# The order of the first loads, and the order of the work, in a gated SSM and MLP kernel with all its gradients

## The chip, the cores and the metric

The kernel runs on one core of a Trainium2 chip, in one launch. The metric is the device time of that launch in microseconds (us), here as the median of several runs. A core has five instruction streams: TensorE (PE, matmuls, with its weight loads shown as PEld), VectorE (DVE), ScalarE (ACT), GpSimd (POOL) and SyncE (SP). Each works through its own list in order. SP, ACT and POOL also issue DMA transfers, each into a queue of its own: SP's is q1, ACT's q10 and POOL's q0 in the profile.

## The reference, cut to what matters

```python
# u: 1 x 2048 x 448, bf16; A, B, C: 448 x 256 complex (six real arrays); w1: 448 x 1792
g = sigmoid((u * gate_w).sum(-1, keepdims=True))
# S4: kernel of the state space model, then a causal convolution over the 2048 steps
dt = exp(log_dt)
K  = einsum("dn,dnl,dn->dl", C, exp(dt * A * l), dt * B).real     # l = 0 .. 2047
a  = irfft(rfft(pad(u)) * rfft(pad(K)))[:2048] + u * Dskip
# MLP with a squared ReLU
b  = relu(u @ w1 + b1) ** 2 @ w2 + b2
out = g * a + (1 - g) * b
# and jax.vjp of out for grad_out: gradients of u, the six parameters, log_dt, Dskip, w1, b1, w2, b2, gate_w
```

The output and the 14 gradients are all written.

## The kernel before

The program is recorded first and ordered afterwards. `build()` calls small helpers (`R.dma`, `R.op`, `mm`, `cp`, `act`, `scaled`, `tt`), and each call leaves a task in the list `R.tasks`: its engine, other engines that could do it, a rank, and what it depends on. 2271 tasks are recorded before. A long packed table of numbers, `PLAN`, then says in which order the tasks are issued, which engine each takes where there is a choice, and where each buffer lies in the one large SBUF array `arena` and in the PSUM array `banks`. So the names `arena` and `banks` in the profile cover nearly all tiles, and the lines of the profile are those of the loop at the end that issues the tasks: L1408 matmul, L1410 transpose, L1412 DMA transpose, L1414 memset, L1416 activation, L1418 copy and DMA, L1420 every other operation (in the changed file each is two lines further down). A transfer that a task list shows waits on the chip only for the buffers that it reads and writes; `R.rel` and `R.dep` (a time and tasks before which a task isn't placed) guided the search that made `PLAN`, and set no wait by themselves.

The stages, in the order in which PE goes through them:

- The 2048 steps of u lie in `U` as 128 partitions x 16 steps x 448 channels. `U` is loaded by 8 transfers of 32 partitions (224 KB each, two halves h and four groups g of partitions), grad_out in `G` by 4 transfers (448 KB each).
- `fwd1(U)` (f1 below): 14 groups of 64 small matmuls against the constant `F1BD`. Each group fills two PSUM banks and is evicted by a copy of 128x1024 into `s`, on ACT or DVE. Each matmul takes all 128 partitions, so it needs all four partition groups of a half.
- `spread`: the constant `M2` (1536 KB) is multiplied by the mask `hm` into `M2x`, in four pieces of 128x3072, on ACT or DVE.
- `fwd2` (f2): 16 groups of 16 matmuls of `M2x` against `s`, evicted into `sp0`. f1 and f2 together are the long Fourier transform of u.
- On DVE meanwhile: 16 products of u with gate_w, summed per step (SCALAR_TENSOR_TENSOR of 128x448); ACT makes the sigmoid g of them; then `DA` = G * g and `DB` = G * (1 - g), 16 pieces of 128x448 each, on DVE or ACT. `db2`, 16 matmuls, sums G * (1 - g) over the steps.
- `pp`: the six parameter arrays in `prm` (224 KB each, read in runs of 512 bytes) are transposed on PE, in six groups of 8 matmuls. DVE and ACT form the powers of the state matrix from them, by eleven squarings one behind another (`lam0`, `lam1`), stored to and loaded from `rec_d`; tables `Y` and `XP` are built of these, `yt` are their transposes on PE.
- `fwd1(DA)` and f2 of it, the product with u's transform and the way back (`i1`, `dk`), the MLP (`h`, `pj`), seven chunks of tables with the kernel K and its gradient, a third f1 at some 616 to 660 us, the way back to y and du, and at the end the parameters' gradients, mostly on DVE.

Around the change, a queue takes its transfers in the order in which its engine issues them. SP issues four of u's loads, then the six parameter loads; ACT gate_w, `F1BD`, the other four of u, two of grad_out's, `negI` and `ident`; POOL two of grad_out's, log_dt, `M2`, later a copy of u to DRAM (`u_d`, from which `xT` is read transposed for the MLP) and the MLP weights `w1`. ACT's computing instructions stand behind its load issues, in the same stream.

Of the kernel before, what the change touches and what calls it, by code (L numbers as in the profile page):

```python
# [1450 lines left out]
```

## Time and profile before

| what | value |
|---|---|
| median of 3 runs | 786.06 us (783.39 to 787.68) |
| the profiled execution | 789.6 us, span of the trace 787.8 us |
| granted TensorE clock, mean | 0.935 |
| PE busy | 649.3 us, 82% of the span |
| DVE, ACT, POOL busy | 564.6, 423.7, 137.5 us |
| moved by DMA | 159.97 MB, mean 203 GB/s |
| first matmul, first eviction | 23.55 us, 30.84 us |

Times in rows of the trace count from the start of its span. A row of the timeline has a start, a length, the engine, the line, the operation with the array written and the array read, and the number of instructions put together; brackets hold the idle time of the engine before it and what ended that. "issue" there means that the profile shows nothing that the engine waited for.

### The profile page before, as it was taken

The page shows a single profiled execution, that of the slowest core. Times are in us where ns is not written, and L with a number is a line of the kernel's source. Part 1 is how long each engine was busy: PE and PEld are TensorE (multiplying, and loading weights), DVE is VectorE, ACT ScalarE, POOL GpSimd, SP SyncE. Part 2 cuts the span into 40 slices and gives each one's busy share as a digit, 9 for nine tenths or more (in the row PEclk, how much of TensorE's full clock was granted, in tenths as well). Part 3 has the DMA queues.
Part 4 walks back from the last instruction along what each step waited for, and adds up shares of the span by engine and source line. Part 5 has one row for each costly group of instructions (what it writes and reads, how often), then busy time and mean ns, then how long its engine had stood idle before and what let it go on. Part 6 is the DMA issues. An engine that isn't in the chain of part 4 may idle for free. (4 is left out here: it accounts for less than half of the span.)

```text
span 787.8 us, 22783 instructions
## 1 busy us (share of the span) xinstructions
PE 649.3 (82%) x10168; PEld 471.6 (60%) x10168; DVE 564.6 (72%) x695; ACT 423.7 (54%) x482; POOL 137.5 (17%) x228
## 2 busy tenths in 40 slices
PE   0368577898978988989899979799899459999797
PEld 0267565565655687766686757687687458444243
DVE  0556688698656679879969959969846226677996
ACT  0268599872734888772664434660266416344136
POOL 3201222122210202011012101300031101222124
PEclk9978999999998999999989989999999659999899
DMA  9945837979535755249674494747979954989995
GB/s 211 285 98 205 308 117 281 312 221 348 144 113 158 186 168 166 85 116 203 104 162 104 91 172 143 191 100 174 245 226 245 333 199 108 319 308 396 308 326 144
DMA packets 157324, 159.97 MB, mean 203 GB/s; under 512 B 94085, under 2 KB 139354, under 8 KB 156074
## 3 DMA queue, kind: packets, MB, share of 16 engines
q1 hardware_dynamic: 137802, 87.89, 43.3%
q0 software_dynamic: 15152, 67.42, 26.0%
q10 hardware_dynamic: 4272, 3.21, 1.8%
q8 instruction: 79, 1.29, 0.7%
q14 instruction: 19, 0.16, 0.1%
HBM read 69.85 MB, written 68.17 MB: 175 GB/s over the span
## 5 line engine op out<-in xcount | busy, mean ns | idle before, releaser
L1408 PE MATMUL banks<-arena 128*32 128x64 bf16 (+10 forms) x9616 | 612.8, 266 | 132.7 <-issue 55.4
L1408 PEld LDWEIGHTS <-arena 128*32 128x32 bf16 (+4 forms) x9612 | 435.2, 121 | 299.3 <-issue 180.7
L1420 DVE TENSOR_TENSOR arena<-arena 128x512 bf16<-128x512 bf16 (+16 forms) x417 | 403.9, 1000 | 69.4 <-ACT arena L1418 25.4
L1418 ACT CAST arena<-banks 128x896 bf16<-128x896 f32 (+7 forms) x270 | 213.5, 835 | 210.8 <-PE banks L1408 192.2
L1416 ACT ACTIVATE arena<-arena 128x672 bf16<-128x672 bf16 (+11 forms) x82 | 105.6, 1333 | 21.6 <-DVE arena L1420 8.8
L1418 ACT COPY arena<-banks 128x2048 bf16<-128x2048 bf16 (+5 forms) x69 | 62.3, 926 | 70.5 <-PE banks L1408 44.1
L1418 DVE CAST arena<-banks 128x896 bf16<-128x896 f32 (+3 forms) x35 | 36.2, 1043 | 69.8 <-PE banks L1408 38.2
L1420 DVE SCALAR_TENSOR_TENSOR arena<-banks,arena 128x448 bf16<-128x448 f32 (+2 forms) x64 | 53.6, 867 | 24.4 <-PE banks L1408 16.9
L1418 POOL DMA_DIRECT2D out_dram<-arena x47 | 25.6, 548 | 108.6 <-ACT arena L1418 73.2
L1410 PE MATMUL banks<-arena 128*128 128x128 bf16 (+1 forms) x552 | 41.7, 234 | 3.0 <-DVE arena L1420 2.1
L1410 PEld LDWEIGHTS <-arena 128*128 128x128 bf16 (+1 forms) x552 | 36.8, 105 | 8.5 <-issue 5.5
L1420 DVE SCALAR_TENSOR_TENSOR arena<-arena 128x448 bf16<-128x448 bf16 (+1 forms) x26 | 20.9, 803 | 20.5 <-DMA arena<-in_A_u_dram 19.6
L1416 ACT ACTIVATE arena<-banks 128x1024 bf16<-128x1024 f32 (+1 forms) x24 | 22.8, 962 | 19.3 <-DMA r_d<-arena 7.2
L1418 POOL DMA_DIRECT2D br_d<-arena x22 | 12.1, 549 | 109.3 <-ACT arena L1418 109.3
L1420 DVE TENSOR_SCALAR arena<-arena 128x448 bf16<-128x448 bf16 (+10 forms) x57 | 25.5, 499 | 1.1 <-ACT arena L1416 0.8
L1420 DVE TENSOR_TENSOR arena<-banks,arena 128x168 bf16<-128x168 f32 (+1 forms) x22 | 13.1, 615 | 16.1 <-ACT arena L1418 15.9
L1418 ACT CAST arena<-arena 128x1792 bf16<-128x1792 f32 x11 | 18.7, 1700 | 3.4 <-DVE arena L1420 3.3
L1414 POOL MEMSET arena<- 128x128 bf16 (+8 forms) x37 | 11.8, 349 | 48.0 <-PE banks L1410 18.5
L1418 POOL DMA_DIRECT2D r_d<-arena x7 | 7.2, 1027 | 57.7 <-ACT arena L1416 43.1
L1418 ACT ACT_TABLE_LOAD x1 | 1.3, 1283 | 29.5 <-DMA arena<-in_A_A_re_dram 29.5
L1418 POOL DMA_DIRECT2D rec_d<-arena x10 | 9.8, 981 | 41.5 <-ACT arena L1418 41.5
L1418 POOL COPY arena<-arena 128x768 bf16<-128x768 bf16 (+1 forms) x8 | 12.1, 1514 | 14.6 <-DMA arena<-rec_d 14.6
(47 smaller groups left out, 102.6 us busy)
## 6 DMA issues: line engine op xcount, KB each, us to landing
arena<-hd SPq DMA_DIRECT2D x12, 896.0 KB, 10.8
r_d<-arena SPq DMA_DIRECT2D x9, 896.0 KB, 5.9
r_d<-arena POOLq DMA_DIRECT2D x7, 896.0 KB, 6.5
arena<-r_d POOLq DMA_DIRECT2D x7, 896.0 KB, 8.1
sp<-arena POOLq DMA_DIRECT2D x6, 896.0 KB, 7.0
hd<-arena POOLq DMA_DIRECT2D x12, 448.0 KB, 7.0
hd<-arena SPq DMA_DIRECT2D x12, 448.0 KB, 5.4
arena<-sp SPq DMA_DIRECT2D x6, 896.0 KB, 8.5
```

The lines of the kernel that those rows point to most:

```text
L1408: fn(out, **kw)
L1410: fn(out, kw["in_"], kw["ident"], **({"tile_position": kw["tile_position"]} if "tile_position" in kw else {}))
L1414: fn(out, kw["value"])
L1416: fn(out, kw.pop("in_"), kw.pop("func"), **kw)
L1418: fn(out, kw["in_"])
L1420: fn(out=out, **kw)
```

## The change

The eight loads of u become the first on SP and on ACT (there behind `F1BD`). gate_w, `hm` and `M2` go to SP behind them, and all six parameter loads to SP. All four loads of grad_out, then log_dt, `ident`, `negI`, and `MI` and `NMI` go to POOL; for the search these are placed behind `uL`, the last of SP's loads of u. The search's costs of an f1 eviction are lowered, and the table `PLAN` is a new one. ACT issues 13 transfers instead of 18, SP 207 instead of 203.

```diff
 PLAN = """
-c-qZc2Xs|cv!2;|X7&!G-Q=cRKp-H!NC4>wp$XD^F9DG%9i&6(9U{FGdWX<EM2a8^gx)nOD1rh~6cK&r
...
+c-qZc3Aj&H*I(0KYrEH-=geb>NGXwUWe9}~Nn|KxC>aXLJVfRxQ!?BJLy@U64;OVag%TM`lcbU~Nzr%C
...
-    R.dma(gwb.v(0, [[1, D]]), DR(gate_w.partition_broadcast(P)), ("ACT",))
     F1 = const("F1BD", q=("ACT",))
     for h in range(2):
         for g in range(4):
             R.dma(U.v(8 * D * h, [[1, 8 * D]], 32 * g, 32), d(u2, (16 * g + 8 * h) * D, [[64 * D, 32], [1, 8 * D]]), ("SP",) if g % 2 else ("ACT",))
+    uL = R.tasks[-3]
+    R.dma(gwb.v(0, [[1, D]]), DR(gate_w.partition_broadcast(P)), ("SP",), rank=0.1)
+    hm = const("hm", dt=fp32, q=("SP",), rank=0.2)
+    M2c = const("M2", q=("SP",), rank=0.3)
+    R.dep = (uL,)
     for g in range(4):
-        R.dma(G.v(...), d(G2, ...), ("ACT",) if g % 2 else ("POOL",))
-    ident = const("ident", q=("ACT",))
-    negI = const("negI", q=("ACT",))
+        R.dma(G.v(...), d(G2, ...), ("POOL",), rank=0.3)
+    R.rank = 1.0
+    MI = const("MI", q=("POOL",), rank=0.8)
+    NMI = const("NMI", q=("POOL",), rank=0.8)
+    ident = const("ident", q=("POOL",))
+    negI = const("negI", q=("POOL",))
+    ldb = R.buf("ldb", 448)
+    R.dma(ldb.v(0, [[1, D]]), DR(A_log_dt.partition_broadcast(P)), ("POOL",))
+    R.dep = ()
     prm = R.buf("prm", 6144)
     for i, src in enumerate(Ap):
-        R.dma(prm.v(...), d(src, ...), ("ACT", "SP"), rank=1.0)
-    ldb = R.buf("ldb", 448)
-    R.dma(ldb.v(0, [[1, D]]), DR(A_log_dt.partition_broadcast(P)), ("POOL",))
-    R.rel = 7.0
-    M2c = const("M2", q=("POOL",))
-    hm = const("hm", dt=fp32, q=("POOL",))
-    MI = const("MI", q=("POOL",))
-    NMI = const("NMI", q=("POOL",))
+        R.dma(prm.v(...), d(src, ...), ("SP",), rank=1.0)
...
             if not runs:
-                t_.dur, t_.alts = 1.4, [(e_, c_, 1.6) for e_, c_, _ in t_.alts]
+                t_.dur, t_.alts = 1.02, [(e_, c_, 1.225) for e_, c_, _ in t_.alts]
```

ACT at the start of the program, before (128x64x16 are evictions of f1, 128x48x64 pieces of M2x, 128x16 the sigmoid, 128x448 pieces of DB or the exponential of log_dt):

```order
L1418 DMA arena<-c_F1BD 128x256
L1418 DMA arena<-in_A_u_dram 32x3584 x3
L1418 DMA arena<-in_grad_out_dram 32x7168
L1418 DMA arena<-c_negI 128x128
L1418 DMA arena<-in_grad_out_dram 32x7168
L1418 ACT_TABLE_LOAD
L1418 CAST arena<-banks 128x64x16
L1418 DMA arena<-c_ident 128x128
L1418 CAST arena<-banks 128x64x16 x4
```

ACT at the same place in the changed program:

```order
L1420 DMA arena<-c_F1BD 128x256
L1420 DMA arena<-in_A_u_dram 32x3584 x4
L1420 ACT_TABLE_LOAD
L1420 CAST arena<-banks 128x64x16 x5
L1418 ACTIVATE arena<-arena 128x48x64 x2
L1420 CAST arena<-banks 128x64x16
L1418 ACT_TABLE_LOAD
L1418 ACTIVATE arena<-arena 128x16
L1420 CAST arena<-banks 128x64x16 x2
L1418 ACTIVATE arena<-arena 128x448 x2
```

Five load issues have left ACT's stream, and after five evictions it takes two pieces of M2x one behind the other. Behind the rows shown follow a table load, one 128x448, the last eviction of f1 that is ACT's, a copy and two more 128x448, and then the evictions of f2.

SP at its start, before:

```order
L1418 DMA arena<-in_A_u_dram 32x3584 x4
L1418 DMA arena<-in_A_A_re_dram 112x4x256
L1418 DMA arena<-in_A_B_re_dram 112x4x256
L1418 DMA arena<-in_A_A_im_dram 112x4x256
L1418 DMA arena<-in_A_C_im_dram 112x4x256
L1418 DMA arena<-in_A_C_re_dram 112x4x256
L1418 DMA arena<-in_A_B_im_dram 112x4x256
L1412 DMA_TRANSPOSE arena<-u_d 128x8x128 x2
```

and in the changed program (c_M is `M2`):

```order
L1420 DMA arena<-in_A_u_dram 32x3584 x4
L1420 DMA arena<-in_gate_w_dram 128x448
L1420 DMA arena<-in_A_A_re_dram 112x4x256
L1420 DMA arena<-c_hm 128x2
L1420 DMA arena<-in_A_B_re_dram 112x4x256
L1420 DMA arena<-in_A_C_re_dram 112x4x256
L1420 DMA arena<-c_M 128x6144
L1420 DMA arena<-in_A_A_im_dram 112x4x256
L1420 DMA arena<-in_A_B_im_dram 112x4x256
L1420 DMA arena<-in_A_C_im_dram 112x4x256
```

M2 now stands behind gate_w, the small mask and three of the parameter loads, and three more stand behind it.

POOL at its start, before:

```order
L1418 DMA arena<-in_grad_out_dram 32x7168
L1418 DMA arena<-in_A_log_dt_dram 128x448
L1418 DMA u_d<-arena 2048x1x64
L1414 MEMSET arena 128x16x64
L1414 MEMSET arena 128x1
L1418 DMA arena<-c_M 128x6144
L1414 MEMSET arena 64x1792
```

and in the changed program (the first u_d transfer writes the pad, the second u itself):

```order
L1416 MEMSET arena 128x16x64
L1420 DMA u_d<-arena 2048x1x64
L1416 MEMSET arena 128x1
L1420 DMA arena<-c_mask 128x4
L1416 MEMSET arena 64x1792
L1420 DMA arena<-in_grad_out_dram 32x7168 x4
L1420 DMA arena<-in_A_log_dt_dram 128x448
L1420 DMA arena<-c_ident 128x128
L1420 DMA arena<-c_negI 128x128
L1420 DMA u_d<-arena 2048x1x448
L1420 DMA arena<-c_NMI 128x256
L1420 DMA arena<-in_B_w_dram 128x3x1792
```

grad_out's four loads follow the memsets, and the copy of u and the MLP weights follow with no load of M2 among them.

Further on, DVE takes two pieces of M2x instead of three, behind 13 of its 16 products of u with gate_w; PE runs the 14 groups of f1(U) back to back, then db2, then f2 and four of the six transposes `pp`, with the other two inside f1(DA) (before, three pp lay inside f1(U) and db2 behind f1(DA)). The first table transposes `yt` are PE's 108th task instead of its 138th: they have moved ahead of the groups `dk`.

More of the change, by code (lines that the diff above doesn't have):

```diff
@@ new lines @@
+p#kKBWJrblPylX*g3u5OL1AbMb)g=#gCcMX)Q6&QClrHQp*XaLmT)<gfZ9+J8pBOc16n~XC<Qg)3MdVCK^-Uqw?iAa5*k5sC<j+Tc_<4_ARaD*1ZWDk!BZFqv+)jS1~YInR)I-a0mfiqyaq;L3n+q>;c6&~RiPtP
+g9%t2#^Vjp9<GB<a4l4VhhYTX3+d1cM&nrQ2~Xhta6L@K-f$z_2P1JfM$;600J_8D7z-7l19X9L*aN!496X2*!a(Q-gJBR1g@<4W^oL<^H$002;8C~-9)m}qFFc8zp&0gonOG7p$EjExOJEr+h1cN~SPnDrN-T{P
+aX6I63OE9;$8m5iR>HY39;RbIxC)12SsVqGF#~SEtFbCp!6)Dv?1@jo6c~m#;sh8CvtSZTglaejCc{nmBvi+-FaW2*V^{;z@nM_}191rU!r3qrYT^ud9B#&1_%6<Y_izx_!P?jx58?N47$3orP#34c2iOPS$9niI
++={p05$uoi;5lf3gRwr&hxPCwJ`MfwX>5oKpfNs!8{jr<glFIxSPcuI39f}T@I0)9=6E}PgzMl1Xo{<#8Qy^(<3?zOEpQRE#7FT?Tn<O^E<A=yU<LHW*7y>%!==y`+u&k&8Scgx;T6~fZ^Ave40ggBa39`_?Qsue
@@ new lines @@
+!d}=79dIkW1>4|N=!l!)e$0X+yd64YC)@?cVGBHfAHhEO6kdZ5;BDxN$DkW_!S1*bKZXbK6YPQUv>y`aLwE>ZhvRqvK7k#ONT1?Cc#luO3H%HW!TWraKf`zVb9@KB#1Hr|e1RYFhkOb@=41R7e!@rKG#=;o;8T7V
+VrV@dg%kWW#?ncAA3oz$ilZd@9P&^yy@t<W8hydvKniW({IrEHqi^9fZ0657FBPFL;cLi81?VIfmQ(N@d;uG|D4m2%-o!uiKK=@}@;L_C!*6jxdYcb&7QV{o`8CdBl)YSxUPqE2`AuGe`}qebP6zlbyu(|u5M53`
+K@lk`uk#jMiraV_{=~0hCT{0VxE*)!LfnO$@jUG0ow$p4;E(VI{|w(?VcN}y_%NSh!eHU!If%e$jKmoHl5-*B8_2Q`V=)d51#@Ep#$zHX=0ztC(=ZRJn26-VRP^{2C*x(9OHw2X)8rdI&B>A~Uvpl08;i-ee7WSu
+e6kz!OA;2B0=ORw;$@P8C8QAU!8~#Ry}W}FG7lpqx9r6ziI(T_O)Ma9;e3pd7jQMl%3@rAak2>GWjTJw=P^M_P@;T`N%AumltQuw@0S;`f_#T7a2cM#AMks;Mqa|Tcox^;1M(BD$1d_RmXuPmhBx4kc!iXf@{~^J
@@ new lines @@
+u#A+YtLaJsDoJJK6<mqsq%^HUBBa$=hSqX<DMeQjQ!cuKgszeZa<q=GmQfN(O1Y^VMUj!GYvn3xNfqcCx?Zl6YiW#(mJU);DoJHI%Wb8TTt^kDot)t+)JATi@42JgNI!55>MXUSCRL@orM9HYjZ%$nkQ#D5Ri}HY
+id2)Ta+6e|`{*92DW|DEwU^3NU2dRz<tw^{>d0L*R_>E=Qj6+RZ5l5(OI@i$4d`Z?C=;ZfOp<yuS)P!FbSq7fRy0-WOCxF`w@7PhDAS~wG?L~rU2d1#WQH`BTcsy8klX1tYAR1kbGk!zNMmXtchGieLrv%#X+d{N
+TWU&oQcKw;&8QvCln14ibd`?ut$ZilWRFDhUGk80m)6ol=E>_aSQg0ud0rltp7Mh9lD#rto|Wh1P3bL<$cwUA7Dyj?RF=pa(pMHrKiMh$<t<q%_t4$6O9skvStjkN6Lp~bX}1iL6*5dZ(-0XdBjj-zDG$(N@{$af
+S@Mdkl9lqZ?2`@Bg*M6>d63r0Q?gdN(k59i-Doa#r%YKbJ?MJ3UuMf@d5GSYhbcqm$hB^+Y?U(-!CT~enM6Ox(^Ao8&^vULo{?AOpd6AP<pX+0&dU3AKz@?ra-BOOPt##}kv@~l+`ICc#Jh8n$0fUG=sihs&(cvz
@@ L462 @@
+Jj#rK3;mf<IrH|$W(MqNm%STgL`q<1$g#}G@I5}@e5d%ZKO;Jnm=W9tyTLIOAP)QY#!Aq$EXe1BV?tSjgLuTpoDTXAYUs=JfzM9IgsUVR128rr?4KCy3+J;l+}Plr$q`BEaU96nmaHk^?ic3vl1V2MC&q^yDIA}j
+H3Ph7gS?s%8`cBMllmuye$(vzvU@^iR7P}0K#3D^T@pj>@d2LDdzlz|b8TRA28DLi&(6%{WpG5MAM8#g&d}A?$#;q^ADbR`I%aUpU|t<_*5(CK3q6-N7~3+4O6lMl9c1&oB(OGkt_=`<j{gNH{-%x
 """
@@ L567, in build @@
             R.dma(U.v(8 * D * h, [[1, 8 * D]], 32 * g, 32), d(u2, (16 * g + 8 * h) * D, [[64 * D, 32], [1, 8 * D]]), ("SP",) if g % 2 else ("ACT",))
-    for g in range(4):
-        R.dma(G.v(0, [[1, LT * D]], 32 * g, 32), d(G2, 16 * g * D, [[64 * D, 32], [1, LT * D]]), ("ACT",) if g % 2 else ("POOL",))
-    ident = const("ident", q=("ACT",))
-    negI = const("negI", q=("ACT",))
+    uL = R.tasks[-3]
[3 more added lines that the diff above has]
+    R.dep = (uL,)
+    for g in range(4):
+        R.dma(G.v(0, [[1, LT * D]], 32 * g, 32), d(G2, 16 * g * D, [[64 * D, 32], [1, LT * D]]), ("POOL",), rank=0.3)
+    R.rank = 1.0
[6 more added lines that the diff above has]
+    R.dep = ()
     prm = R.buf("prm", 6144)
     for i, src in enumerate(Ap):
-        R.dma(prm.v(1024 * i, [[256, 4], [1, 256]], 0, 112), d(src, 0, [[N, 112], [112 * N, 4], [1, N]]), ("ACT", "SP"), rank=1.0)
-    ldb = R.buf("ldb", 448)
-    R.dma(ldb.v(0, [[1, D]]), DR(A_log_dt.partition_broadcast(P)), ("POOL",))
-    R.rel = 7.0
-    M2c = const("M2", q=("POOL",))
-    hm = const("hm", dt=fp32, q=("POOL",))
-    MI = const("MI", q=("POOL",))
-    NMI = const("NMI", q=("POOL",))
+        R.dma(prm.v(1024 * i, [[256, 4], [1, 256]], 0, 112), d(src, 0, [[N, 112], [112 * N, 4], [1, N]]), ("SP",), rank=1.0)
     R.rel, R.dep = 0.0, ()
```

73 lines of the change are left out of this document (29 added, 44 removed).

## The prediction

> **What bounds the kernel now.** I read the page's engine totals first, then a table by stretches of the span, then the waits, the first 82 us of the timeline and the DMA issues. The totals, and TensorE's busy tenths in 40 slices of 19.7 us:
>
> ```profile
> PE 649.3 (82%) x10168; PEld 471.6 (60%) x10168; DVE 564.6 (72%) x695; ACT 423.7 (54%) x482; POOL 137.5 (17%) x228
> PE   0368577898978988989899979799899459999797
> ```
>
> TensorE (PE) carries the kernel on the average, but its row is weak at the left edge. The stretches (stretch, length, then busy time of PE, weight loads, DVE, ACT, POOL; granted TensorE clock, DMA share, GB/s):
>
> ```profile
> 0.00:23.50 23.50, 0.00 (x0) 0.00 (x0) 3.74 (x12) 0.00 (x0) 7.87 (x17) 1.00 0.95 212
> 23.50:58.60 35.10, 18.64 (x920) 17.61 (x921) 18.10 (x55) 17.39 (x16) 5.58 (x7) 0.85 0.75 191
> 58.60:81.20 22.60, 18.13 (x280) 17.02 (x279) 14.79 (x23) 19.82 (x24) 3.86 (x8) 0.85 0.53 215
> 81.20:111.20 30.00, 17.39 (x899) 16.25 (x898) 19.72 (x20) 19.78 (x18) 5.82 (x8) 0.94 0.58 204
> 160.00:600.00 440.00, 399.48 (x5535) 304.75 (x5534) 347.22 (x382) 246.83 (x278) 64.84 (x109) 0.96 0.67 167
> ```
>
> Until 23.5 PE and ACT do nothing, while the DMA engines are 95% busy. From 160 to 600 PE works 399 of 440 us. So the start is bound by loads, the middle by PE. Which loads, the waits tell (total, times, longest):
>
> ```profile
> ACT L1418 <- DMA arena<-in_A_A_re_dram: 29.5, 1, 29.5
> PE banks L1408 <- issue: 55.4, 23, 4.6
> PE banks L1408 <- DMA arena<-in_A_u_dram: 23.5, 1, 23.5
> ```
>
> and the timeline (start, length, engine, what; in brackets the idle time before it):
>
> ```profile
> 15.95 0.32 ACTq L1418 DMA_DIRECT2D arena<-in_grad_out_dram  x1
> ...
> 23.55 2.24 PE L1408 MATMUL banks<-arena 128*32 128x64 bf16 x128 [23.55 <-DMA arena<-in_A_u_dram]
> ...
> 29.19 0.32 ACTq L1418 DMA_DIRECT2D arena<-in_grad_out_dram  x1
> 29.54 1.28 ACT L1418 ACT_TABLE_LOAD   x1 [29.54 <-DMA arena<-in_A_A_re_dram]
> ...
> 30.84 1.93 ACT L1418 CAST arena<-banks 128x1024 bf16<-128x1024 f32 x2
> 31.90 3.68 PE L1408 MATMUL banks<-arena 128*32 128x64 bf16 x222 [6.12 <-ACT arena L1418]
> ...
> 39.29 2.21 PE L1408 MATMUL banks<-arena 128*32 128x64 bf16 x128 [3.71 <-issue]
> ...
> 58.65 0.96 PE L1408 MATMUL banks<-arena 128*64 128x224 bf16 x16 [0.24 <-ACT arena L1418]
> ...
> 59.91 0.58 ACT L1416 ACTIVATE arena<-arena 128x448 bf16<-128x448 bf16 x1
> ...
> 61.18 0.96 ACT L1418 COPY arena<-arena 128x448 bf16<-128x448 bf16 x1
> ...
> 63.11 13.72 PE L1408 MATMUL banks<-arena 128*64 128x224 bf16 x224 [3.50 <-DVE arena L1420]
> ```
>
> The first transform of u starts at 23.55, when u is there. ACT, which evicts it, still stands in front of its own load issues: grad_out's second load goes out only at 29.19, and the first eviction starts at 30.84. The second transform (f2) starts at 58.65 and, after a wait for a piece of the spread matrix M2x, in earnest at 63.11.
>
> **The change, part by part.** *u first.* The DMA of the first 60 us (queues q0 for POOL, q1 for SP: packets, MB, share; then single loads: size, median us from issue to landing):
>
> ```profile
> DMA packets 7272, 11.70 MB, mean 195 GB/s; under 512 B 2992, under 2 KB 5936, under 8 KB 7008
> ...
> q0 software_dynamic: 1312, 6.68, 38.6%
> q1 hardware_dynamic: 5088, 2.82, 26.1%
> ...
> arena<-c_M POOLq DMA_DIRECT2D x1, 1536.0 KB, 23.1
> arena<-in_A_u_dram SPq DMA_DIRECT2D x4, 224.0 KB, 10.3
> ...
> arena<-in_A_B_im_dram SPq DMA_DIRECT2D x1, 224.0 KB, 22.0
> ```
>
> u is 8 x 224 KB = 1.84 MB. At the 212 GB/s of the first stretch that is 8.7 us, and the first issue lies near 1 us. grad_out's loads now all stand on POOL behind its memsets; the dependence on u's last load is one that only the order's search sees (a load into another buffer gets no wait for it), so they will still overlap u's tail. I take u in at 13.5, between 9.7 (alone) and 23.5 (as now): nearer the lower end, as M2 and two of grad_out's loads no longer share its time. PE then starts some 10 us earlier. ACT, with five load issues left and none behind a full queue, evicts from about 15 instead of 30.8.
>
> *M2 late.* This takes most of it back. M2 stood on POOL, issued at 5, and took 23.1 us: in at 28.2. Now it is seventh of SP's loads behind u, gate_w and three parameter loads. ACT's instructions are in order: after five evictions come two M2x pieces that need M2, so ACT stops there; DVE stops too, after 13 of its 16 products for the gate. When is M2 in? Before it or beside it go u 1.84 MB, grad_out 1.84, the copy of u to DRAM 1.84, u's pad 0.26, MLP weights 1.38, three parameters 0.69, M2 itself 1.57 and small ones of about 0.3: 9.7 MB. At 212 GB/s this ends at 46; at 258 (the 11.70 MB, if nearly all of it is in when the last parameter load, issued at 23.4, lands 22.0 later at 45.4) at 38. M2 need not be the last of them, so I take 38, with 28 (as before) and 45.4 as ends. A load's place in SP's queue is what I price here, not its size.
>
> The Trainium skill's page "DMA: Bandwidth & Descriptors", section "Queues, rings and completion order", says that a DMA engine takes turns between the queues that have work, a whole packet each. The q0 and q1 rows agree in kind: q1 moved 5088 packets for 2.82 MB, q0 1312 for 6.68 MB. By that rule M2, behind 512-byte parameter packets that each give way to a large one, comes late: the first rival below.
>
> *From M2 to f2.* What ACT must still do, with rows for each kind (busy, mean ns, idle before):
>
> ```profile
> L1418 ACT CAST arena<-banks 128x1024 bf16<-128x1024 f32 x12 | 11.8, 1014 | 11.6 <-PE banks L1408 11.6
> ...
> L1416 ACT ACTIVATE arena<-arena 128x3072 bf16<-128x3072 bf16 x1 | 2.9, 2873 | 0.0
> L1416 ACT ACT_TABLE_LOAD x2 | 2.6, 1283 | 0.0
> ...
> L1420 DVE TENSOR_SCALAR arena<-arena 128x3072 bf16<-128x3072 bf16 x2 | 2.0, 1013 | 0.0
> ```
>
> Two M2x pieces 5.75 (one more on ACT than now, at 2.87 where DVE pays 1.01), four evictions 4.06, two table loads 2.57, the sigmoid 0.2, three activations 1.74: 14.3 us to the last eviction of f1(u). PE then does db2 (16 matmuls that used to come after the transform of the scaled gradient) ahead of f2; it needs the last scaled rows, another copy 0.96 and two activations 1.16 on ACT. So f2 starts 16.4 + about 0.4 after M2: at 38 + 16.8 = 54.8. It was 63.11 with one of its 16 groups already done (0.96): 8.3 - 1.0 = 7.3 us earlier.
>
> *db2 and the parameter transposes.* They change places: db2 leaves the time after f1 of the gradient, three of six transposes move from the wait for M2x to behind f2.
>
> ```profile
> L1408 PE MATMUL banks<-arena 112*128 112x112 bf16 x24 | 3.1, 335 | 0.0
> L1408 PE MATMUL banks<-arena 128*1 128x448 bf16 x16 | 3.2, 352 | 0.0
> ```
>
> 3.2 against 3.1: nothing.
>
> *The waits for "issue".* PE stops 23 times, 55.4 us in all, in runs of 128 matmul records between stops (39.29 above). The number of matmuls is the same, so I leave them: 0, with the saving of one or two stops (4 us each, the longest is 4.6) as a gain that lighter traffic behind 40 us may give, and the same as a loss. The Trainium skill's page "Runtime: NRT & Kernel Launch", section "Instruction fetch mechanics", says instructions come in 16 KiB blocks by DMA, and that crossing a block is mostly hidden; the 55.4 us speak against "hidden" in this kernel. By the page the term is 0 as well.
>
> *The planner's costs* (1.02 and 1.225 for an eviction) are the measured 1014 ns and nearly DVE's; they execute nothing.
>
> *The order searched anew.* Instructions are the same up to a few moved between engines. PE is busy 399 of 440 us, so there is little to win in the middle: 0, between -8 and +8, which is what two stops for issue each way would make. In the stretch 81 to 111 PE works 17.4 of 30: the gradient's transform shares it with the recurrence of powers on DVE. A denser DVE order can win there; I take 2 of PE's 12.6 idle us.
>
> Sum against the profiled execution: 789.6 (span 787.8) - 7.3 - 2 = 780.3. That execution lies 3.5 above the median of the three runs shown, 786.06, so 776.8; I say 777.
>
> **The rivals.** *M2 last.* If M2 comes when the parameters came, at 45.4, f2 starts at 62.2, 0.9 earlier, less 1.0 for the group done early: no gain. With 2 us from the denser order it is 784. For it: q1's packets are small and many. Against it: half the parameters now stand behind M2.
>
> *Slower: the table transposes come too early on PE.* The first tables' transposes now stand ahead of the gradient's kernel products (dk), some 30 groups earlier in PE's order. They need the last of eleven steps on DVE:
>
> ```profile
> 161.77 1.08 DVE L1420 SCALAR_TENSOR_TENSOR arena<-arena 128x896 f32<-128x896 f32 x1
> ...
> 204.49 1.95 PE L1410 MATMUL banks<-arena 128*128 128x128 bf16 x32
> ```
>
> and these matmuls stand between on PE (140 to 206 us):
>
> ```profile
> L1408 PE MATMUL banks<-arena 128*128 128x256 bf16 x152 | 18.6, 273 | 0.0
> L1408 PE MATMUL banks<-arena 128*32 128x448 bf16 x260 | 16.4, 353 | 2.3 <-DMA arena<-hd 2.3
> ```
>
> PE now gets there at 204.5, some 40 us after that step. Of the 93 us from the end of the gradient's f1 (111.2) to there, what is now put behind takes dk 16.4, 88 MLP matmuls of 256 columns at 18.6 / 152 = 0.12 each 10.8, ten of 448 some 2, and db2 3.2: 60 are left. The gradient's f1 would start at 54.8 + 15.9 for f2 + 4.1 for four transposes, near 75, and end, with the other two inside it, near 75 + 30 + 2 = 107, so PE arrives at 167. With tables some 8 us after the last step, that is at 170, it waits 3 if the recurrence is no earlier than now. DVE's order puts all the scalings of the gradient (27, nearly in a row) ahead of the parameters' first products, which can make it later. The case decides when the wait passes the 9 gained and the 4 that a measurement tells; at 18 us it costs 9 net: 795. Against it: DVE waits for f2 in that stretch anyway, and other work between the steps is moved too.
>
> *More kept.* If M2 comes at 28.2 as before, f2 starts at 45.0, 18.1 - 1.0 earlier: 789.6 - 17.1 - 2 - 3.5 = 767. For it: SP's own bytes up to M2 are only 3.3 MB. Against: 5 MB go beside them on POOL's queue.
>
> *It does nothing.* The gain at f2 can be eaten by a chain that starts elsewhere: the recurrence needs the parameters, of which three are now behind M2. If it starts no earlier than now, PE finds its gain again as a wait before the tables: 786.
>
> **How the numbers follow.** A measurement of this kernel can tell about 0.5%, 3.9 us: faster is below 782.1, slower above 790.0. Chances: forecast (771 to 782) 0.40; more kept (762 to 771) 0.17; M2 last or nothing gained (782 to 790) 0.25; slower 0.18. Faster is therefore 0.40 + 0.17 and a part of the border, 0.58; same 0.24; slower 0.18. The range reaches from 763 (the kept case and a stop saved) to 791, leaving out about 0.2; the forecast's own is 771 to 782.
>
> **What will show it.** u in by 12 to 16, first eviction before 18; ACT idle behind its fifth eviction until M2 is in, at 34 to 42; f2's first group 16 to 18 us later; a start of the gradient's transform near 75 against 81. If PE's first table transposes have a long wait ahead of them, the slower rival is at work. The forecast is wrong if M2 is in before 32 or after 44, or if the gain at 111 us is not that at 600.

## The result and the profile after

The changed kernel takes 807.6 us (median of 4 runs, 805.0 to 815.2) against 785.3 us for the kernel before beside it: ratio 1.0298, interval 1.0217 to 1.0379. It is slower by about 3%; the forecast was 777 us. The profiled execution took 805.1 us, its span is 803.4 us.

The totals of the page of the changed kernel and TensorE's busy tenths (40 slices of 20.1 us):

```profile
PE 642.4 (80%) x10168; PEld 465.8 (58%) x10168; DVE 566.9 (71%) x692; ACT 421.6 (52%) x488; POOL 138.0 (17%) x226
PE   1367776898883699989899999499968389949886
```

TensorE does no more work than before (649.3 us there); it stands still for longer. The granted clock of this execution was lower on the mean, 0.915 against 0.935, but no engine's busy time grew by more than 2.3 us, so the clock is not where the time went. The stretches, of the changed kernel (the columns are those of the table before):

```profile
0.00:23.50 23.50, 4.67 (x270) 4.50 (x274) 6.69 (x19) 3.31 (x3) 10.68 (x21) 0.89 0.94 232
81.20:111.20 30.00, 23.69 (x748) 21.00 (x748) 20.23 (x21) 20.38 (x18) 6.52 (x12) 0.80 0.62 217
111.20:160.00 48.80, 34.04 (x376) 22.48 (x372) 47.44 (x44) 44.37 (x43) 9.13 (x12) 0.93 0.81 267
160.00:600.00 440.00, 381.69 (x5424) 290.48 (x5423) 336.60 (x367) 237.64 (x277) 59.57 (x102) 0.95 0.64 161
```

and the third of these stretches in the kernel before:

```profile
111.20:160.00 48.80, 40.98 (x466) 27.54 (x462) 39.89 (x33) 43.18 (x43) 13.27 (x19) 0.97 0.85 278
```

Up to 111 us TensorE is ahead: 4.67 us of work by 23.5 us instead of none, 23.69 instead of 17.39 between 81 and 111. From 111 to 160 it does 34.04 instead of 40.98, while VectorE is busy for 47.44 of 48.80 us. From 160 to 600 it does 381.69 instead of 399.48.

These stretches are cut by the clock, and the two orders do different work in them. A place that both pass with nearly the same work left is the last 128x224 matmul of the third long transform, at 663.9 us before and 664.8 us in the changed kernel. The rest of the span, first before, then changed:

```profile
663.90:787.80 123.90, 112.20 (x799) 50.65 (x798) 98.42 (x158) 49.01 (x77) 29.96 (x51) 0.96 0.83 288
664.80:803.40 138.60, 115.47 (x840) 52.83 (x839) 98.19 (x161) 50.20 (x76) 34.47 (x57) 0.96 0.83 283
```

So in these two executions the lead of the start is gone at that place, and 14.7 of the 15.6 us of loss come behind it, in what is called the tail below.

The start, from the timeline of the changed kernel:

```profile
12.26 4.01 PE L1410 MATMUL banks<-arena 128*32 128x64 bf16 x221 [12.26 <-DMA arena<-in_A_u_dram]
13.54 1.01 ACT L1420 CAST arena<-banks 128x1024 bf16<-128x1024 f32 x1 [7.23 <-PE banks L1410]
38.95 5.60 ACT L1418 ACTIVATE arena<-arena 128x3072 bf16<-128x3072 bf16 x2 [7.92 <-DMA arena<-c_M]
38.97 1.95 DVE L1422 TENSOR_SCALAR arena<-arena 128x3072 bf16<-128x3072 bf16 x2 [12.74 <-DMA arena<-c_M]
50.97 18.68 PE L1410 MATMUL banks<-arena 128*32 128x64 bf16 x331 [1.55 <-issue]
```

u is in at 12.26, the first eviction starts at 13.54, ScalarE and VectorE wait for M2 until 38.95. The last row runs from the end of f1 through db2 into f2, whose first matmul is at 54.6.

The waits of TensorE in the whole span, the two largest and that for hd (total, times, longest):

```profile
PE banks L1410 <- issue: 81.4, 28, 8.9
PE banks L1410 <- DVE arena L1422: 30.2, 18, 11.2
...
PE banks L1410 <- DMA arena<-hd: 7.8, 1, 7.8
```

The waits for issue were 55.4 us before. Of the 26 us added, 13 lie in the first 58.6 us (22.1 against 8.9), where M2 is waited for in any case, 9 between 160 and 300 (11.8 against 3.1) and 11 between 480 and 600 (16.5, 2.2 of it on another line, against 5.3); elsewhere they fell a little. They are waits for TensorE's own instructions, which come by DMA; the page has their queue:

```profile
q8 instruction: 79, 1.29, 0.6%
```

In the packed trace, each of the 27 waits for issue over 0.8 us ends 1.2 to 1.6 us after a packet of 16,384 bytes of q8 has landed (the one that ends at 513.17 us, for example, after a packet that landed at 511.9).

The 11.2 us for VectorE is the longest of its kind. The timeline around it:

```profile
244.21 0.73 SPq L1420 DMA_DIRECT2D arena<-dk_d  x1
247.84 4.49 DVE L1422 TENSOR_TENSOR arena<-arena 128x4096 bf16<-128x4096 bf16 x2 [3.70 <-DMA arena<-dk_d]
248.31 1.10 POOL L1420 DMA_DIRECT2D r_d<-arena  x1 [9.13 <-DMA arena<-dk_d]
253.94 0.58 ACTq L1420 DMA_DIRECT2D arena<-dk_d  x1
254.62 0.97 ACT L1420 CAST arena<-banks 128x448 bf16<-128x448 f32 x2 [12.86 <-DMA r_d<-arena]
257.27 4.30 DVE L1422 TENSOR_TENSOR arena<-arena 128x4096 bf16<-128x4096 bf16 x3 [4.94 <-DMA arena<-dk_d]
259.67 1.41 PE L1410 MATMUL banks<-arena 128*32 128x42 bf16 x109 [11.21 <-DVE arena L1422]
```

The two DMAs out of dk_d are the third and fourth of the four loads into dKc, the table of the gradient's kernel. Each writes every fourth partition (32 of 128, 42 x 112 elements). The built program lets the first of them wait for twelve DMA semaphores and one of VectorE:

```
DMA arena<-dk_d 32x42x112 [waits DMAHW2_49,DMAHW1_49,DMAHW3_49,DMASW7_49,DMAHW4_49,DMASW5_49,DMAHW5_49,DMASW4_49,DMAHW6_49,DMASW2_49,DMAHW7_49,DMASW1_49,DVE_49]
```

The other three wait for ten, nine and four semaphores, VectorE's and ScalarE's among them. What was said ahead of the prediction, that a transfer waits only for the buffers that it reads and writes, does not hold for these four; why the program was built with these waits is not shown. VectorE, ScalarE and POOL behind the loads wait for them in their turn (the brackets of the rows above). So each of the four is close to a full stop. At 244.21 the third goes out; VectorE may begin its next products only when it has landed (247.84); the fourth goes out only when those products (to 252.33) and the store of POOL, which lands at 253.79, have ended, and ScalarE stands behind its issue for 12.86 us; VectorE starts again at 257.27, and TensorE, which hangs on that product, at 259.67. The kernel before has the same four loads.

### The profile page after: what moved, and what is told of

Read it like the earlier page. It is cut to its first block, busy times and chain, and to the rows that moved or that the text cites. A ratio compares the mean times of both kernels' runs of the same rounds, so it can differ in the third digit from the quotient of the medians.

```text
span 803.4 us, 22792 instructions
## 1 busy us (share of the span) xinstructions
PE 642.4 (80%) x10168; PEld 465.8 (58%) x10168; DVE 566.9 (71%) x692; ACT 421.6 (52%) x488; POOL 138.0 (17%) x226
## 4 chain that ended last, share of the span: by engine, by line
PE 61%; issue 14%; DVE 13%; DMA 8%; ACT 4%; SPq 0%; POOL 0%; DVEq 0%; ACTq 0%; POOLq 0%
PE banks L1410 57%; DVE arena L1422 11%; PE banks L1412 4%; ACT arena L1420 3%; DMA arena<-hd 2%; DMA arena<-dk_d 2%; DMA r_d<-arena 1%; DVE arena L1420 1%; ACT arena L1418 1%; DMA arena<-in_A_u_dram 1%; DMA arena<-db_d 1%; DMA arena<-k_d 0%; DMA arena<-c_F1BD 0%; DMA arena<-u_d 0%; DMA k_d<-arena 0%
## 5 line engine op out<-in xcount | busy, mean ns | idle before, releaser
L1410 PE MATMUL banks<-arena 128*32 128x64 bf16 (+9 forms) x9616 | 607.4, 267 | 153.9 <-issue 81.4
L1410 PEld LDWEIGHTS <-arena 128*32 128x32 bf16 (+4 forms) x9612 | 430.4, 120 | 319.0 <-issue 189.2
L1422 DVE TENSOR_TENSOR arena<-arena 128x512 bf16<-128x512 bf16 (+15 forms) x419 | 403.2, 995 | 42.8 <-DMA arena<-dk_d 20.6
L1418 ACT ACTIVATE arena<-arena 128x672 bf16<-128x672 bf16 (+11 forms) x84 | 103.5, 1272 | 22.2 <-DMA arena<-c_M 7.9
L1420 ACT COPY arena<-banks 128x2048 bf16<-128x2048 bf16 (+5 forms) x69 | 58.9, 881 | 88.5 <-PE banks L1410 66.8
L1420 DVE CAST arena<-banks 128x896 bf16<-128x896 f32 (+4 forms) x39 | 40.8, 1051 | 77.9 <-PE banks L1410 45.0
L1422 DVE TENSOR_SCALAR arena<-arena 128x448 bf16<-128x448 bf16 (+10 forms) x53 | 26.0, 557 | 16.6 <-DMA arena<-c_M 12.7
L1422 DVE SCALAR_TENSOR_TENSOR arena<-arena 128x448 bf16<-128x448 bf16 (+1 forms) x26 | 20.8, 801 | 17.2 <-DMA arena<-in_gate_w_dram 16.6
L1418 ACT ACTIVATE arena<-banks 128x1024 bf16<-128x1024 f32 (+1 forms) x28 | 25.0, 910 | 12.7 <-PE banks L1410 12.7
L1420 DVE COPY arena<-banks 128x2048 bf16<-128x2048 bf16 (+1 forms) x9 | 10.4, 1151 | 25.8 <-PE banks L1412 25.8
L1420 POOL DMA_DIRECT2D hd<-arena x16 | 12.3, 768 | 82.8 <-ACT arena L1420 81.4
L1420 ACT COPY arena<-arena 128x256 bf16<-128x256 bf16 (+3 forms) x23 | 13.0, 579 | 9.1 <-DMA arena<-rec_d 7.5
L1420 POOL DMA_DIRECT2D r_d<-arena x10 | 8.8, 882 | 44.9 <-ACT arena L1418 20.2
```

Of the source, the lines that this page charges most:

```text
L1410: fn(out, **kw)
L1418: fn(out, kw.pop("in_"), kw.pop("func"), **kw)
L1420: fn(out, kw["in_"])
L1422: fn(out=out, **kw)
```

## The experiments

All ratios are to the kernel before, run beside (its median is 785.3 us beside the changed kernel and 789 to 791 beside the others). "Order" in the table stands for all that `PLAN` holds: the order, the engines and the addresses.

| kernel | order | loads at the start | loads into dKc | ratio, interval |
|---|---|---|---|---|
| before | before's | before's | by partitions | 1 |
| e1_loads | before's | the change's | by partitions | 0.9923 (0.9888 to 0.9959) |
| e2_order | the change's | before's | by partitions | 1.0376 (1.0310 to 1.0442) |
| after | the change's | the change's | by partitions | 1.0298 (1.0217 to 1.0379) |
| e4_before_rows | before's | before's | by columns | 0.9843 (0.9784 to 0.9903) |
| e3_after_rows | the change's | the change's | by columns | 0.9927 (0.9891 to 0.9963) |
| f1_before_loads_rows | before's | the change's | by columns | 0.9766 (0.9706 to 0.9827) |

**The loads alone, and the order alone.** e1 takes the order, engines and addresses of before and puts the loads at its head in the change's sequence and on its queues:

```diff
-    order = planned(R)
+    order = moved(R, planned(R))
...
+    head = [("SP", us[0]), ("ACT", ld["F1BD"][0])] + [x for a, s in zip(ua, us[1:] + [None]) for x in (("ACT", a), ("SP", s)) if x[1] is not None]
+    head += [("SP", i) for i in (ld["gwb"][0], prm[0], ld["hm"][0], prm[1], prm[2], ld["M2"][0], prm[3], prm[4], prm[5])]
+    late = [("POOL", i) for i in ld["G"][:4] + [ld["ldb"][0], ld["ident"][0], ld["negI"][0]]]
...
+    order[k:k] = [i for _, i in late]
+    order[:0] = [i for _, i in head]
```

> The order, engines and addresses of before, with only the first loads placed as in the change (u first and alone on SP and ACT, gate_w, M2 and the parameters behind it on SP, grad_out, log_dt, ident and negI on POOL). If the loss lies in the order searched anew, this keeps the start's gain: first matmul near 12, M2 in near 38, f2 some 6 to 9 us earlier, 776 to 782. If the 9 us that the start gains are always used up behind it, because DVE and ACT bound the stretch from 100 to 160 us whatever the order, it comes out at 784 to 788, as before. If the placing of the loads itself does the harm, it is slower than 790.

e2 is the converse: the changed order, with the loads in before's sequence and on before's queues.

```diff
+    pool = [("POOL", G[0]), ("POOL", G[2]), ("POOL", ld["ldb"][0]), ("POOL", ld["M2"][0]), ("POOL", ld["hm"][0])]
+    act = [("ACT", i) for i in [ld["gwb"][0], ua[0], ld["F1BD"][0]] + ua[1:] + [G[1], ld["negI"][0], G[3], ld["ident"][0]]]
+    sp = [("SP", i) for i in us + prm]
...
+    order[:0] = [i for _, i in pool[:3] + act + sp]
```

> The order, engines and addresses of the change, with the first loads put back as they were before (gate_w, half of u, half of grad_out, negI and ident on ACT; M2 and half of grad_out on POOL; the parameters alone on SP). If the loss lies in the order of the work behind the start, it is at least as slow as the change, 805 to 818 (the start's 9 us are lost as well). If the loads do the harm (M2 late, parameters late), it returns to 784 to 790.

The loads alone make the kernel faster, 0.9923; the order alone makes it slower, 1.0376. The two together, 0.9923 x 1.0376 = 1.0296, are the change (1.0298), well within the intervals. The rival that loads, or M2 behind them, do the harm is refuted. e1's 782.9 us fell between its first two forecasts (776 to 782, 784 to 788): most of the start's gain is kept, not all. e2 has the changed kernel's long wait too; the largest of TensorE's waits of e2 from 160 to 300 us:

```profile
PE banks L1448 <- DVE arena L1460: 15.7, 3, 12.0
```

**The stops taken away.** e3 (on the changed kernel) and e4 (on the kernel before) cut the same data, over the same four queues, by columns: each load writes all 128 partitions of ten or eleven of the 42 columns.

```diff
-        R.dma(dKc.v(0, [[112, 42], [1, 112]], c4, 32, ps=4), d(dk_d, 112 * c4, [[D, 32], [32 * D, 42], [1, 112]], [("dk",)]), ...)
+        k0, kk = (0, 11, 22, 32)[c4], (11, 11, 10, 10)[c4]
+        R.dma(dKc.v(112 * k0, [[112, kk], [1, 112]]), d(dk_d, 32 * D * k0, [[112, 128], [32 * D, kk], [1, 112]], [("dk",)]), ...)
```

> The change, with the four loads of the kernel's gradient (dk_d into dKc) cut by columns of 112 (all 128 partitions, 11, 11, 10 and 10 of 42 pieces each) instead of by every fourth partition. The bytes, their runs of 224 bytes and their places are the same. In the change each of the four loads waits for every engine's earlier work, and everything behind waits for it: PE stands 11.2 us at the last one, behind a store of 5 us. If these four full stops are a main part of the loss, they go and the time falls by 10 to 18: 788 to 798. If the loss is PE's waits for its instructions (81 us against 55) elsewhere, it stays within 4 us, 802 to 808.

> Before, with the same four loads cut by columns. The stops in before cost PE 4.3 and 3.9 us at two of the four, and DVE and ACT 3 to 7 us at each. If they bind there too, 775 to 781; if PE's own work hides them, 783 to 787.

In the changed kernel the cut is worth 0.9927 / 1.0298 = 0.964, about 29 us, more than forecast; in the kernel before 0.984, about 12 us. By the intervals these are good to some 7 and 5 us. The profiled executions of the changed kernel and e3 differ by less, 803.4 against 786.3 us: the one was among the shortest of its kernel, the other among the longest. The first load of e3 waits for five semaphores, all of DMA queues, instead of thirteen, and none of the four waits for VectorE or ScalarE any more:

```
DMA arena<-dk_d 128x11x112 [waits DMAHW3_49,DMAHW2_49,DMAHW5_49,DMASW4_49,DMASW1_49]
```

TensorE's waits from 160 to 300 us, first of the changed kernel, then of e3:

```profile
PE banks L1410 <- DVE arena L1422: 14.6, 3, 11.2
PE banks L1410 <- issue: 11.8, 5, 4.6
```

```profile
PE banks L1411 <- issue: 5.3, 3, 2.0
PE banks L1411 <- ACT arena L1421: 2.2, 4, 1.1
```

26.4 us in the two largest rows become 7.5, and TensorE waits for VectorE no more in this stretch. That it is the waiting and not the transfer shows in the landings that the trace has for both, of the changed kernel and of e3 (KB each, median us from issue to landing; between 205 and 262 us):

```profile
arena<-dk_d POOLq DMA_DIRECT2D x1, 294.0 KB, 3.7
arena<-dk_d SPq DMA_DIRECT2D x1, 294.0 KB, 3.5
```

```profile
arena<-dk_d POOLq DMA_DIRECT2D x1, 308.0 KB, 5.4
arena<-dk_d SPq DMA_DIRECT2D x1, 280.0 KB, 5.1
```

Cut by columns they take longer, beside other traffic, and cost less.

**What a stop costs.** Two edits of the changed kernel leave the stops in. g2 puts the store that was in flight ahead of the fourth stop (248.31 above) behind it; g4 puts the second to fourth load right behind the first.

```diff
+    for i, j in ((515, 957),):                            # g2: store of r2_d behind the fourth load
+    for i, j in ((956, 954), (955, 954), (957, 956)):     # g4: the loads together
         order.remove(i)
         order.insert(order.index(j) + 1, i)
```

> The changed kernel with one edit: the store into r2_d on POOL's queue that was issued at 248.31 us and landed at 253.79 us is put behind the last of the four loads into dKc, which was issued at 253.94 us. Theory that a load into every fourth partition stops the program until every transfer in flight has landed, so that its price is the latest of these: the last stop is then issued some 4 to 5 us earlier, TensorE's wait there (11.2 us) falls to 5 to 7 us, and the time falls by 4 to 6 us, 1.022 to 1.026. Rival, that the price is the load's own transfer and the work behind it, whatever is in flight: no change, 1.030.

> The changed kernel with one edit: the four loads into dKc follow each other at the place of the first (218 us), instead of at 218, 233, 244 and 254 us. Theory that each stop costs the draining of what is in flight and the refilling of the engines behind it: the second to fourth find nothing in flight but the load before, and cost about 3.7 us each (the landing of one); the four together hold TensorE for 12 to 16 us in one piece instead of 27 us of waits between 160 and 300 us, and the time falls by 8 to 14 us, 1.012 to 1.020. Rival, that the stop's price is a fixed one per load, or that the engines starve longer in one piece than in four: 1.025 to 1.040.

g2: 1.0181 (1.0120 to 1.0243), below both forecasts, with an interval that overlaps the changed kernel's; the profiled span, 803.5 us, is the same as the changed kernel's, and the wait hardly moved. From its timeline:

```profile
245.10 4.49 DVE L1446 TENSOR_TENSOR arena<-arena 128x4096 bf16<-128x4096 bf16 x2 [4.38 <-DMA arena<-dk_d]
249.67 0.58 ACTq L1444 DMA_DIRECT2D arena<-dk_d  x1
255.60 1.59 PE L1434 MATMUL banks<-arena 128*32 128x42 bf16 x126 [10.56 <-DVE arena L1446]
```

10.56 us instead of 11.21. With the store gone the stop waits for VectorE's two products (245.10 + 4.49 = 249.59), which had ended 1.6 us before the stop in the changed kernel. I had taken the store for the price of the stop; it was only the last of several things that it waits for, by 1.6 us. g4: 1.0116 (1.0063 to 1.0168), below the forecast band of 1.012 to 1.020 by a hair and clear of the changed kernel. Its waits from 160 to 300 us:

```profile
PE banks L1434 <- DVE arena L1446: 8.5, 1, 8.5
PE banks L1434 <- issue: 5.3, 3, 2.3
```

One piece of 8.5 us instead of 14.6 in three, and 5.3 instead of 11.8 for instructions. The rival, a fixed price per load, is refuted. The rest agrees with a price of draining what runs and filling up again, paid once where the four stand together; by g2 it does not hang on one transfer. Why the waits for instructions halve as well is not shown.

**What the new order loses beside the stops.** With the cut in both, the changed order stands at 0.9927 and before's, with the same loads, at 0.9766 (f1). 

> The kernel before with two edits: the change's placement of the loads (which alone gave 0.992) and the four loads into dKc cut by columns (which alone gave 0.984). If the two gains lie in different places of the program (the first ends at 111 us, the second lies between 215 and 260 us), they add: 0.977, about 770 us. The rival is that the lead from the loads is spent in a wait behind 260 us that does not move with it, as in the changed order: then no better than 0.984, about 776 us.

The two gains add, as the first theory said (0.9923 x 0.9843 = 0.9767). So the changed order costs 0.9927 / 0.9766 = 1.0165, 13 us (to some 5), even without stops. The traces show where: the third long transform ends at 645.5 us in f1 and at 645.0 in e3, so the orders are level there, and the tail behind it is longer. First f1, then e3:

```profile
645.50:768.90 123.40, 111.73 (x799) 50.43 (x798) 98.58 (x158) 48.99 (x77) 29.88 (x51) 0.95 0.84 289
645.00:786.30 141.30, 117.89 (x840) 53.12 (x840) 98.51 (x161) 50.19 (x76) 34.45 (x57) 0.93 0.82 278
```

VectorE works for as long in both; TensorE works 6 us longer and waits 20.2 us instead of 8.7. This holds in every trace: with before's order (five kernels) the tail takes 123 to 125 us, with the changed order (eight kernels, f3 below apart) 138 to 141, whatever the loads and the stops are. Four edits of e3 looked for the 13 us; only f3 is in the tail. The largest of TensorE's waits of e3 from 480 to 600 us, and in its last stretch:

```profile
PE banks L1411 <- issue: 16.0, 3, 8.1
```

```profile
PE banks L1411 <- DMA arena<-hd: 8.7, 2, 7.8
```

f2 moves two loads of the buffer rc (from r_d in DRAM) and a store to dh_d, 896 KB each on POOL's queue, away from the DMA transposes into the buffer zT:

```diff
+    for i, j in ((817, 1560), (853, 1560), (878, 1614)):
+        order.remove(i)
+        order.insert(order.index(j) + 1, i)
```

> The changed kernel with the loads into dKc cut by columns (0.9927 of the kernel before), and in addition two loads of rc and one store of dh_d on POOL's queue moved behind the two spots where the DMA transposes into zT run (477 to 489 us and 550 to 570 us in that kernel). Theory that TensorE's waits for its own instructions between 480 and 600 us (17.3 us there) come from the transposes and POOL's transfers of 896 KB running at the same time: the transposes then land in 6 to 8 us, the issue waits of this stretch fall below 10 us, and the time falls by 5 to 10 us, 0.980 to 0.987. Rival, that the instruction blocks would wait there whatever POOL moves: no change, 0.993. Second rival: rc then comes late for its first use, and the time rises by as much as rc is late, up to 10 us.

1.0011 (0.9975 to 1.0047): slower than e3 by some 7 us, the second rival. From f2's waits of the same stretch and its timeline:

```profile
PE banks L1435 <- DVE arena L1447: 10.6, 4, 8.7
PE banks L1435 <- issue: 9.0, 2, 5.7
PE banks L1437 <- issue: 3.2, 1, 3.2
```

```profile
571.26 0.58 POOL L1445 DMA_DIRECT2D arena<-r_d  x1
582.56 2.95 DVE L1447 SCALAR_TENSOR_TENSOR arena<-banks,arena 128x1024 bf16<-128x1024 f32 x3 [12.33 <-DMA arena<-r_d]
583.84 8.44 PE L1435 MATMUL banks<-arena 128*128 128x256 bf16 x69 [8.65 <-DVE arena L1447]
```

The waits for instructions fall from 17.3 (16.0 and a 1.3 on another line) to 12.2, less than forecast, so the crowd has a part in them, but rc, loaded late, holds up VectorE for 12.33 and TensorE for 8.65 us.

f3 works on the tail: the buffer hs is loaded from hd in DRAM while pg (1792 KB), brr and ST are loaded too. It puts pg and brr behind the load of rw, and ST behind hs:

```diff
+    for i, j in ((2089, 2150), (2149, 2150), (2148, 2066), (2147, 2066)):
+        order.remove(i)
+        order.insert(order.index(j) + 1, i)
```

> The changed kernel with the loads into dKc cut by columns (0.9927), and in addition the load of pg (1792 KB) and of brr put behind the load of rw, and the two loads of ST behind the load of hs, so that hs has the DMA engines nearly to itself near 700 us. Theory that the 7.8 to 8.7 us for which TensorE waits for hd in the last stretch are the time by which these transfers hold back hs: the wait falls below 2 us and the time by 5 to 9 us, 0.981 to 0.987. Rival, that the last stretch is bound by VectorE and by ST or pg coming later: the wait moves to these, and the time stays, 0.993, or rises by up to 5 us.

0.9894 (0.9843 to 0.9946), and the wait in the last stretch of f3 is

```profile
PE banks L1435 <- DMA arena<-hd: 2.1, 1, 2.1
```

so the crowd behind hs made most of the wait, and the tail is shorter, 133.0 us against 141.3 in e3. The time is between the two forecasts: 0.9927 to 0.9894 is 2.6 us, and whether these are real the intervals leave open.

f4 loads hm and M2 ahead of the parameters:

```diff
+    pr = [i for i in order if tname(T[i]) == "prm"][0]
+    for n in ("hm", "M2"):
+        before_task(order, [i for i in order if tname(T[i]) == n and T[i].used[0] == "SP"][0], pr)
```

> The changed kernel with the loads into dKc cut by columns (0.9927), and in addition the loads of hm and M2 put ahead of the six loads of parameters on SP's queue. M2, for which ScalarE and VectorE wait until 39 us, then lands near 28 us, and f2 begins 8 to 10 us earlier, near 45 us. If what is won at the start reaches the end, the time falls by 6 to 10 us, 0.980 to 0.985. Rival, that the parameters (which now land some 4 us later) hold back the chain of the tables, or that VectorE between 111 and 160 us swallows the lead as it did in the changed kernel: below 3 us, 0.989 to 0.993.

0.9946 (0.9903 to 0.9989): nothing, as the rival had it. M2 came 12 us earlier, but f1 was then bound by TensorE's own instructions, as f4's timeline shows:

```profile
26.75 1.95 DVE L1447 TENSOR_SCALAR arena<-arena 128x3072 bf16<-128x3072 bf16 x2 [1.24 <-DMA arena<-c_M]
34.67 2.21 PE L1435 MATMUL banks<-arena 128*32 128x64 bf16 x128 [3.98 <-issue]
```

f2's first matmul came at 51.95 instead of 54.60, 2.7 us, and these did not reach the end.

g3 takes four operations that write the table W4 from VectorE to POOL, to relieve the stretch from 111 to 160 us:

```diff
+    for i in (379, 380, 381, 382):
+        T[i].used = ("POOL", T[i].used[1])
```

> The changed kernel with the column cut (0.9927), and in addition the four casts into W4 (1.08 us each on VectorE, between 109 and 128 us, used first at 187 us) on POOL, which is busy 8 of the 49 us from 111 to 160 us. Theory that VectorE, busy 47 of these 49 us, bounds the stretch and swallows the lead of the start: TensorE's waits there (13.4 us for ScalarE and VectorE) fall by 3 to 4 us, and as there is no stop behind any more, the time falls by 2 to 4 us, 0.988 to 0.990. Rival, that ScalarE (44 of 49 us) bounds it as much, or that POOL's queue is held up by the casts: 0.991 to 0.997.

0.9984 (0.9941 to 1.0028): no gain, and slightly above even the rival's band. The stretch in g3:

```profile
111.20:160.00 48.80, 34.68 (x357) 21.62 (x352) 45.41 (x39) 43.52 (x42) 15.33 (x17) 0.86 0.77 260
```

VectorE gave up a little (45.41 against 46.76 in e3), TensorE gained nothing (34.68 against 35.83). What holds TensorE there is not shown; VectorE and ScalarE are both nearly full, so relief of the one may only show the other. So, by the traces, the 13 us lie in the tail. Part of them is the wait for hd, which f3 shortens by 6.6 us; the rest is longer work of TensorE and short waits for VectorE (8.6 us in e3, nine times), and what makes these is open: the order was not taken apart piece by piece.

**The best version.** f1 (before's order, the change's loads, the cut by columns) takes 769.8 us (766.6 to 774.4), faster than both kernels. g1 adds M2 early:

```diff
-    head += [("SP", i) for i in (ld["gwb"][0], prm[0], ld["hm"][0], prm[1], prm[2], ld["M2"][0], prm[3], prm[4], prm[5])]
+    head += [("SP", i) for i in (ld["gwb"][0], ld["hm"][0], ld["M2"][0], *prm)]
```

> The best kernel so far (the kernel before with the change's placement of the loads and the column cut, 0.9766), and in addition hm and M2 loaded ahead of all six parameters on SP's queue. In the changed kernel with the column cut the same edit brought M2's halves forward by 9 us and f2 by only 2.7 us, since TensorE's waits for its own instructions (four of 4 to 6 us between 16 and 44 us) then bound f1, and nothing of it reached the end (0.9946 against 0.9927). Theory that the lead survives where VectorE does not swallow it between 111 and 160 us, as in this order: 0.973 to 0.975, 2 to 3 us less. Rival, that the parameters come later and hold back the tables: 0.977 to 0.980.

0.9750 (0.9699 to 0.9801), 771.0 us: at the edge of the theory's band, and not to be told from f1.

## Why the prediction was wrong

*u first: right.* u in at 13.5 was forecast, 12.3 was measured; eviction "from about 15", measured 13.54.

*M2 late, from M2 to f2: right in its numbers, in part by luck.* M2 at 38 forecast, 38.95 measured; f2 at 54.8 forecast, 54.6 measured. The 7.3 + 2 us were there at 111 us: f1 of the gradient ended 9 us earlier (102.4 against 111.2). But ScalarE's work behind M2 was not alone on the way to f2: with M2 in 12 us earlier (f4) f2 began only 2.7 us earlier, because TensorE's waits for its instructions, forecast as 0, were nearly as long. That two paths ended together was luck. M2 came later than its own bytes on SP's queue would make it, and most of that lies ahead of its transfer:

```profile
10.33 11.29 SPq L1420 DMA_DIRECT2D arena<-c_M  x1
```

SP stood at this issue for 11.29 us, behind three parameter loads; in f4, where M2 goes out ahead of all six, the issue took 0.49 us at 6.71 us. The rule on turns between queues of "DMA: Bandwidth & Descriptors" in the Trainium skill would make M2 late too. No run here tells it from the wait at the issue, and the packet counts of q0 and q1 shown in the prediction do not test it. The first rival, M2 at 45.4, was too late.

*db2 and the parameter transposes: nothing: right.* db2 takes 3.2 us in both (111.1 to 114.3 before, 51.5 to 54.7 in the changed kernel).

*The waits for issue: 0, one or two stops either way. This term was mis-sized.* They grew by 26 us, 81.4 against 55.4. Those of the start lie beside the wait for M2; of the 9 added from 160 to 300 us most go with the stops (11.8 in the changed kernel, 5.3 in e3); how much of those from 480 to 600 us (16.5 against 5.3) reaches the end is not shown. The section "Instruction fetch mechanics" of "Runtime: NRT & Kernel Launch" in the Trainium skill says that crossing a block of instructions is mostly hidden. Here it is not: the longest wait is 8.9 us, at a place where a transpose and two transfers of 896 KB run together.

*The order searched anew: 0, between -8 and +8. This is the step that failed.* It measured 1.0376 alone, 30 us. The argument was that TensorE is busy 399 of 440 us, so that there is little to win. That bounds the gain and not the loss: TensorE can lose what any other engine makes it wait. A row of the kernel before would have warned, among the waits from 160 to 300 us:

```profile
DVE arena L1420 <- DMA arena<-dk_d: 17.5, 4, 6.1
```

VectorE waited four times for the loads out of dk_d. They were stops there already, and cost 12 us (e4). A new order puts other work around the stops, and g2 and g4 agree with a stop costing what it drains. Of the 30 us, 30 - 13 = 17 are dearer stops (29 - 12 of the cut, the same sum from the other side), and 13 lie in the tail. Each part is good to some 5 to 8 us. In the single profiled executions the stops weigh less and the tail more: up to the end of the third transform the cut saves 19.8 us in the changed order (664.8 to 645.0) and 12.9 in before's (663.9 to 651.0), and the tail is 14.7 us longer.

*The rivals.* The slower rival had the right sign and the wrong place: the first table transposes came to TensorE near 171 us, as early as feared (167), and did not wait. Of the conditions named at the end, "if the gain at 111 us is not that at 600" is the one that was met: 9 us ahead at 102 had become 1 behind after the four stops (the second 256 of the 128x42 matmuls end at 270.1 against 269.0) and 2 behind when the third f1 begins (614.5 against 612.3).

*The sum:* loads -6 (e1), order +30 (e2), together +24; measured +23.4 (0.0298 x 785.3).

## What to carry to other kernels

A share of busy time near 90% says how little an order can win in a stretch, not how much it can lose. Before an order is moved, look for instructions that wait for many queues at once and that everything behind waits for; they can be dear in one order and cheap in another. Taking the stops away, by writing all partitions in place of every fourth, was worth 12 us in one order and 29 in the other, against the 6 that the new loads gained. Compare two orders at a place where the same work is left, and not by the clock alone: so the loss in the tail shows. When one edit brings a new sequence of loads and a new order together, run each alone: here the one gained 6 us and the other lost 30.

## What was not expected of the hardware

The two loads into dKc whose landing the trace has in both kernels land 1.6 and 1.7 us later when cut by columns (5.1 and 5.4 against 3.5 and 3.7 us), and the kernel is still about 29 us faster: here a DMA's duration says little of its cost. The timeline at the longest wait of TensorE for its own instructions in the changed kernel:

```profile
499.44 3.97 SPq L1414 DMA_TRANSPOSE arena<-arena  x1
499.96 0.54 POOL L1420 DMA_DIRECT2D arena<-r_d  x1 [4.33 <-DVE arena L1422]
500.49 0.54 POOL L1420 DMA_DIRECT2D dh_d<-arena  x1
513.17 1.55 PE L1410 MATMUL banks<-arena 128*32 128x42 bf16 x119 [8.94 <-issue]
516.05 0.32 SPq L1420 DMA_DIRECT2D dh_d<-arena  x1
```

A DMA transpose with two transfers of 896 KB issued right behind it landed 16.6 us after its issue at 499.44, and the store of its result goes out at 516.05. With little beside it, a transpose of the same kind issued at 515.64 us in e3 landed after 6.1 us.
